# An attention and MLP kernel on one core: block 1's products during the first solve, merges interleaved on four row groups, values scaled on ScalarE, short solve steps fused

## Chip, core and metric

The kernel runs on one core of a Trainium2 chip. The metric is the device time of one execution in microseconds (us). TensorE (PE) multiplies, VectorE (DVE) and ScalarE (ACT) work on tiles elementwise, GpSimd (POOL) does the same on SBUF, and SyncE (SP) issues the DMAs.

## The reference, cut to what matters

Three layers one after the other: a delta-rule attention over 768 time steps for 4 batches of 8 heads of 48 numbers, a Fourier mixing with an MLP, and a gated MLP. The change touches the attention alone:

```python
k_n = k / (np.linalg.norm(k, axis=-1, keepdims=True) + 1e-06)
state = np.zeros((B, H, D, D))
for t in range(S):
    kt, vt, bt = k_n[:, :, t], v[:, :, t], beta[:, :, t, None]
    y[:, :, t] = np.einsum('bhd,bhde->bhe', q[:, :, t], state)
    v_old = np.einsum('bhde,bhd->bhe', state, kt)
    state = state + bt[:, :, :, None] * np.einsum('bhd,bhe->bhde', kt, vt - v_old)
```

## The kernel before

**Tiling.** Time is cut into 12 chunks of 64 steps for each of 4 batches: 48 chunks `bc`, in an order (`SEQ`) that staggers the batches by four. Two heads share the 128 partitions, so a chunk has four head pairs. Eight chunks make a block; there are six blocks. Inside a chunk the recurrence becomes a unit triangular system. Its inverse is made of two 32x32 triangles, inverted on DVE for a whole block at once (`solve`), and an off-diagonal 32x32 part made from two products on PE (`merge`).

**Stages of a chunk.** `stage_a` loads `kq` (448 KB), takes `k k^T` and `k q^T` on PE into PSUM (line 201), and moves them to the tile `gak`: ACT copies the `k k^T` half in two parts (`copy_g`, lines 191 and 192), DVE masks the `q` half (line 205). `stage_b` loads values `kv` and `qt`, scales the values by the norms of `k` on POOL (line 313), multiplies by the inverse `TT` (line 316) and copies the result to `WU` on ACT (line 321). `stage_c` forms `cw` (lines 332 and 333). `stage_d` takes the output and the new state (lines 345 and 347) and copies them on ACT (lines 358 and 362); it is the recurrence itself.

**Solve.** Line 219 forms `Cc` from the products, lines 226 and 232 scale it by mask and `d` (for blocks 1 to 5 line 226, the tile `dm`, runs on POOL), line 236 transposes it into `T`. Then 30 elimination steps follow, each of two products (line 252) and two additions (line 255) on halves of the rows. Line 271 scales, lines 275 to 277 transpose the result into `T1` and `Tc`. `norms` makes the inverse norms: for block 0 from squares summed on PE, for blocks 1 to 5 from a load `kn`, squared on ACT (line 142) and summed on DVE (line 144), then a root and eight small DVE operations (lines 146 to 153).

**Merge.** For eight head pairs a merge takes 16 products of 32x32 (line 291) into PSUM, ACT negates them into `zs` in two halves (line 296) and copies the diagonal blocks of `Tc` to `TT` (line 298); 16 more products (line 301) and two copies (line 303) complete `TT`. One merge serves two chunks; four merges make a block.

**Order.** The first solve is written out ahead of everything. While it runs, PE does 26 products of 128x512 that nothing reads (`busy(CF["keep"], 512)`, line 407). All later calls are events with a key in units of a chunk: they are emitted in that order with a priority, and a scheduler in the compiler, which simulates the program, sets the final order on each engine. `CF["pin"]` names operations that keep their place in program order. Block 1's `stage_a` may come no earlier than key -4, behind the first solve. The queue of SP is in order, and `kq` has five buffers. When the last solve is done, buffers of the attention are given up and the first weights of the MLP are loaded; the MLP stages follow.

```python
for j in range(1, NB):
    a0 = 8 * j - LM - NS - (8 + NA - 1) // NA
    at(max(a0 - CF["nl"], -LM), "N", norms, j)
```

Of the kernel before, what the change touches and what calls it, by code (L numbers as in the profile page):

```python
# [7 lines left out]
F32 = mybir.dt.float32  # L8
# [12 lines left out]
C = 64  # L21
# [23 lines left out]
    kq=5, kv=2, mb=2, cvd=3, cve=2, kn=4, sv="hhhhhd", pin=574,  # L45
    warm=10, keep=26, dfs=2, tn=2, early=4, ahead=1,
# [14 lines left out]
class Kernel:  # L61
    def __init__(self, tc, a):
        self.tc, self.nc, self.a, self.first = tc, tc.nc, a, None
# [10 lines left out]

    def load(self, out, in_):

        ins = self.nc.sync.dma_start(out=out, in_=in_)
        if self.first is not None:
            dep = mybir.DependencyInfo(mybir.DependencyClass.NoSync, mybir.DependencyReason.DATA)
            self.tc.add_manual_dep(ins.ins, self.first.ins.name, dep, reason="issue order")  # L80
        return ins
# [13 lines left out]
    def attention(self, cp, pg, pe, p, x, filler, after_solves):  # L95
# [17 lines left out]

        def norms(blk):
            if blk in normed:
                return
            normed.add(blk)
            s = slice(blk * 32, blk * 32 + 32)
            n0 = pe.tile([128, 32], F32, name="n0")
            n1 = pe.tile([128, 32], F32, name="n1")  # L120
            if blk == 0:
                ss = self.bank("pc", [128, 32])
                for i in range(2):
                    k2 = pe.tile([128, 1056], F32, name="Ts", bufs=CF["mb"])[:112, :1024]
                    nc.scalar.activation(k2, gas["k"][i].rearrange("p a b c -> p (a b c)"), AF.Square)
                    for g in range(16):
                        for r, q in ROWS:
                            nc.tensor.matmul(
                                ss[q, i * 16 + g : i * 16 + g + 1], lhsT=k2[r, g * C : g * C + C], rhs=one[r], start=True, stop=True
                            )  # L130
            else:
                ss = pe.tile([128, 32], F32, name="ss")
                w = 32 // CF["kn"]
                if blk == 1:
                    kn1 = p.tile([128, 4, HP, GA], F32, name="gak", bufs=3).rearrange("p a b c -> p (a b c)")
                for i in range(0, 32, w):
                    if blk == 1:
                        kn = kn1[:, i * D : (i + w) * D]
                    else:
                        kn = pe.tile([128, w * D], F32, name="kn", bufs=2)  # L140
                    self.load(out=kn, in_=a["kn"][blk, :, i : i + w].rearrange("p w d -> p (w d)"))
                    self.pin(nc.scalar.activation(kn, kn, AF.Square), blk)
                    kn = kn.rearrange("p (w d) -> p w d", d=D)
                    self.pin(nc.vector.tensor_reduce(out=ss[:, i : i + w], in_=kn, axis=AX.X, op=ADD), blk)
            nc.scalar.sqrt(n0, ss)
            nc.vector.tensor_scalar_max(n0, n0, 1e-30)
            nc.vector.reciprocal(n1, n0)
            nc.vector.tensor_mul(n1, n1, ss)
            nc.vector.tensor_add(n1, n1, n0)
            nc.vector.tensor_scalar(out=n_all[:, s], in0=n1, scalar1=0.5, scalar2=1e-6, op0=MUL, op1=ADD)  # L150
            nc.vector.reciprocal(n1, n_all[:, s])
            nc.vector.tensor_mul(n0, n1, bt[:, s])
            nc.vector.tensor_mul(d_all[:, s], n0, n1)
# [39 lines left out]

        def stage_a(bc):
# [12 lines left out]
        def solve(blk, nsl):  # L207

            Cc = pe.tile([128, 32, 32], F32, name="Cc")
            dm = pe.tile([128, 32, 32], F32, name="dm")  # L210
            d = d_all[:, blk * 32 : blk * 32 + 32]
            dT = pe.tile([128, 32], F32, name="dT", bufs=2)
            if blk == 0:
                for i in range(4):
                    copy_g(both0(i, C), pairs0("k", i))
            gs = [gas[blk * 8 + h4 * 4, 4][:, :, :, C : 2 * C].rearrange("p a b c -> p (a b) c") for h4 in range(2)]
            n = 32 // len(gs)
            for i, g in enumerate(gs):
                nc.vector.scalar_tensor_tensor(
                    out=Cc[:, :, n * i : n * i + n].rearrange("p c g -> p g c"),  # L220
                    in0=g[:, :, 32:], scalar=mk[:, 3 * C : 3 * C + 1], in1=g[:, :, :32], op0=MUL, op1=ADD,
                )
            if blk == 0:
                norms(0)
            nc.vector.transpose(out=dT, in_=d)
            (nc.gpsimd if blk else nc.vector).tensor_tensor(
                out=dm,
                in0=mk[:, 3 * C + 2 :].unsqueeze(2).to_broadcast([128, 32, 32]),
                in1=d.unsqueeze(1).to_broadcast([128, 32, 32]),
                op=MUL,  # L230
            )
            nc.vector.tensor_mul(Cc, Cc, dm)
# [3 lines left out]
            self.pin(nc.vector.transpose(out=T, in_=Cc), 16 + blk)  # L236
# [19 lines left out]

            for k in range(1, 31):
# [9 lines left out]
            for i, op in enumerate(steps):  # L267
                if i and i * nsl // len(steps) != (i - 1) * nsl // len(steps):
                    yield
                outer(*op)  # L270
# [6 lines left out]
            nc.vector.transpose(out=T1[:, 16:], in_=Tr[:, 16:])  # L277
            Tts[blk] = (Tc, T1)

        def merge(g8):  # L280

            blk, o = g8 // 4, (g8 % 4) * 8
            Tc, T1 = Tts[blk]
            tt = TT[g8 % NTT]
            z = self.bank("pz", [128, 2, 8, 32])
            qs = [slice(32 * u, 32 * u + 32) for u in range(4)]
            lo, up = qs[::2], qs[1::2]
            ga = [gas[g8 * 2 + g // 4][:, g % 4] for g in range(8)]
            for g in range(8):
                for h in range(2):  # L290
                    nc.tensor.matmul(  # L291
                        z[up[h], 0, g], lhsT=ga[g][lo[h], C + 32 : 2 * C], rhs=T1[lo[h], :, o + g], start=True, stop=True
                    )
            zs = p.tile([128, 8, 32], F32, name="zs", bufs=2)
            for h in range(2):
                nc.scalar.mul(zs[up[h]], z[up[h], 0], -1.0)
            for us in up + lo:
                nc.scalar.copy(out=tt[us, :, us], in_=Tc[us, o : o + 8])
            for g in range(8):
                for h in range(2):  # L300
                    nc.tensor.matmul(z[lo[h], 1, g], lhsT=zs[up[h], g], rhs=tt[up[h], g, up[h]], start=True, stop=True)
            for h in range(2):
# [698 lines left out]
```

## Time and profile before

| | us |
|---|---|
| median of three runs | 953.75 |
| lowest and highest | 952.13, 956.86 |
| the profiled execution | 958.1 |
| its span, first to last instruction | 956.3 |
| PE busy | 915.2 (96%) |
| DVE busy | 562.6 (59%) |
| ACT busy | 405.6 (42%) |
| POOL busy | 204.5 (21%) |

The attention fills the span to about 348 us, the MLP layers the rest. Busy shares are means over stages with different limits. A busy PE is not a PE at its peak: the records of a product run until its modelled end. A product of 32-bit numbers shows as two records.

### The profile page before, as it was taken

The numbers are of one execution on the slowest core, as the hardware profiler recorded it, in microseconds if no ns is written. First come the engines' busy times: TensorE is split into PE (matmuls) and PEld (weight loads), VectorE is DVE, ScalarE is ACT, GpSimd is POOL, SyncE is SP. The second block draws the span as 40 slices with busy tenths as digits, with TensorE's granted clock in tenths as the row PEclk, the third lists the DMA queues.
The fourth block names the chain that finished last, engine by engine and source line by source line (L and its number), as shares of the span: only waits on it lengthen the run. The fifth ranks groups of instructions, "written<-read, shape, count | busy, mean of one in ns | idle before, by whom it ended". The sixth has DMA issues, their size and how long they took to land.

```text
span 956.3 us, 18756 instructions
## 1 busy us (share of the span) xinstructions
PE 915.2 (96%) x7360; PEld 865.5 (91%) x7360; DVE 562.6 (59%) x1675; ACT 405.6 (42%) x1002; POOL 204.5 (21%) x198
## 2 busy tenths in 40 slices
PE   7989879999998998999999999999999999999998
PEld 7468769989998987899999999999989999899898
DVE  3967999988887489774559522322273352443521
ACT  3156566868887655422225221111252342332421
POOL 2011022122115215422124100000072132132221
PEclk7878969979997999999999999999999999999999
DMA  9069935723353254000130000000020100000001
GB/s 251 11 168 237 241 102 150 205 80 85 94 164 89 56 175 168 1 1 1 40 128 32 1 1 1 1 1 17 25 75 8 43 1 25 25 1 25 25 1 50
DMA packets 51593, 67.11 MB, mean 70 GB/s; under 512 B 28945, under 2 KB 41970, under 8 KB 51506
## 3 DMA queue, kind: packets, MB, share of 16 engines
q1 hardware_dynamic: 51506, 65.92, 24.3%
q8 instruction: 58, 0.95, 0.4%
q14 instruction: 29, 0.24, 0.1%
HBM read 61.19 MB, written 4.72 MB: 69 GB/s over the span
## 4 chain that ended last, share of the span: by engine, by line
PE 73%; DVE 11%; ACT 5%; DMA 4%; issue 4%; POOL 2%; SPq 0%; ACTq 0%; POOLq 0%; DVEq 0%
PE bankY L665 13%; PE bankX L650 12%; PE bankX L758 10%; PE bankY L778 5%; PE bankX L744 5%; PE bankX L719 4%; PE bankY L345 3%; PE bankY L316 3%; PE bankY L332 3%; PE bankY L347 3%; PE bankX L201 2%; DMA w<-in_w_dram 2%; PE bankZ L291 2%; POOL w L583 2%; DVE Ts L255 2%
## 5 line engine op out<-in xcount | busy, mean ns | idle before, releaser
L650 PE MATMUL bankX<-uh,w 128*128 128x384 f32 x576 | 162.1, 343 | 2.5 <-ACT w L582 1.4
L665 PE MATMUL bankY<-w,hh 128*128 128x384 f32 x576 | 137.6, 340 | 2.1 <-POOL w L583 1.3
L656 DVE SCALAR_TENSOR_TENSOR hl<-bankX,hh 128x384 fp32r<-128x384 f32 x96 | 53.2, 554 | 139.7 <-ACT hh L655 139.6
L655 ACT ACTIVATE hh<-bankX 128x384 fp32r<-128x384 f32 x96 | 47.0, 489 | 173.5 <-PE bankX L650 173.4
L650 PEld LDWEIGHTS bankX<-uh,w 128*128 128x128 f32 x576 | 104.8, 188 | 5.8 <-ACT w L582 3.2
L665 PEld LDWEIGHTS bankY<-w,hh 128*128 128x128 f32 x576 | 102.8, 188 | 5.3 <-POOL w L583 3.0
L758 PE MATMUL bankX<-ws,vh 128*128 128x384 f32 x384 | 98.6, 337 | 0.0
L650 PE MATMUL bankX<-ul,w 128*128 128x384 f32 x288 | 97.1, 337 | 0.0
L665 PE MATMUL bankY<-w,hl 128*128 128x384 f32 x288 | 84.1, 339 | 1.8 <-DVE hl L656 1.8
L766 DVE TENSOR_TENSOR g<-bankX,bsb 128x384 f32<-128x384 f32 x32 | 17.8, 558 | 101.7 <-PE bankX L758 101.7
L313 POOL TENSOR_TENSOR gak<-gak,n_all 128x192 f32<-128x192 f32 x48 | 38.4, 805 | 181.5 <-DMA gak<-in_kv_dram 128.2
L255 DVE TENSOR_TENSOR Ts<-Ts,tm 128x110 f32<-128x110 f32 (+31 forms) x325 | 76.0, 270 | 0.9
L345 PE MATMUL bankY<-WU,gak 128*112 128x96 f32 (+1 forms) x384 | 72.8, 278 | 1.1 <-ACT x L362 1.0
L252 DVE TENSOR_TENSOR tm<-Ts 128x110 f32<-128x110 f32 (+31 forms) x325 | 70.3, 254 | 0.8
L758 PEld LDWEIGHTS bankX<-ws,vh 128*128 128x128 f32 x384 | 69.1, 188 | 0.0
L347 PE MATMUL bankY<-Sb,cw 112*112 112x96 f32 (+1 forms) x352 | 66.2, 271 | 2.1 <-DVE cw L333 2.1
L758 PE MATMUL bankX<-ws,vl 128*128 128x384 f32 x192 | 64.3, 337 | 0.0
L345 PEld LDWEIGHTS bankY<-WU,gak 128*112 128x112 f32 (+1 forms) x384 | 54.8, 185 | 3.5 <-ACT x L362 1.4
L665 PEld LDWEIGHTS bankY<-w,hl 128*128 128x128 f32 x288 | 52.8, 188 | 2.8 <-DVE hl L656 2.7
L769 POOL TENSOR_TENSOR gl<-g,gh 128x384 fp32r<-128x384 f32 x32 | 32.4, 1013 | 105.3 <-ACT gh L768 88.1
L650 PEld LDWEIGHTS bankX<-ul,w 128*128 128x128 f32 x288 | 54.2, 188 | 0.1
L321 ACT COPY WU<-bankY 64x384 f32<-64x384 f32 x96 | 45.3, 472 | 20.3 <-PE bankY L316 19.0
(164 smaller groups left out, 1917.1 us busy)
## 6 DMA issues: line engine op xcount, KB each, us to landing
kq<-in_kq_dram SPq DMA_DIRECT2D x40, 448.0 KB, 6.6
qt<-in_qt_dram SPq DMA_DIRECT2D x48, 196.0 KB, 2.7
gak<-in_kv_dram SPq DMA_DIRECT2D x48, 192.0 KB, 3.6
w<-in_w_dram SPq DMA_DIRECT2D x24, 384.0 KB, 8.4
out_dram<-ot SPq DMA_DIRECT2D x24, 192.0 KB, 2.0
kn<-in_kn_dram SPq DMA_DIRECT2D x16, 192.0 KB, 3.5
s<-in_wi_dram SPq DMA_DIRECT2D x6, 512.0 KB, 4.0
cvd<-in_ws_dram SPq DMA_DIRECT2D x12, 192.0 KB, 2.4
```

What stands on the lines that cost most here:

```text
L252: nc.vector.tensor_tensor(out=tm, in0=x.to_broadcast(sh), in1=y.to_broadcast(sh), op=MUL)
L255: nc.vector.tensor_add(o, o, tm)
L321: nc.scalar.copy(out=o_, in_=pb[hs])
L345: nc.tensor.matmul(pd[:m, hp], lhsT=ak[:, hp, :m], rhs=u[:, hp], start=True, stop=(c == 0))
L347: nc.tensor.matmul(pd[:m, hp], lhsT=cw[:, hp, :m], rhs=sb[:, hp], start=False, stop=True)
L650: nc.tensor.matmul(ph, lhsT=w1[f][i][:, c * 128 : c * 128 + 128], rhs=cur[k][:, c], start=(c + j == 0), stop=(c == 2 and j == 2))
L655: nc.scalar.activation(hh, ph, AF.Relu)
L656: nc.vector.scalar_tensor_tensor(out=hl, in0=ph, scalar=0.0, in1=hh.bitcast(F32), op0=MAX, op1=SUB)
L665: nc.tensor.matmul(acc[t], lhsT=hx[i][:, t * 128 : t * 128 + 128], rhs=w2[e][k], start=(e == 0 and j == 0), stop=(e == 11 and j == 2),)
L744: nc.tensor.matmul(pu, lhsT=wi[2 * c][i][:, f * 128 : f * 128 + 128], rhs=xT[hf][k][:, c], start=(c + j == 0), stop=(c == 2 and j == 2),)
L758: nc.tensor.matmul(pv, lhsT=vn[i][:, s, f * 128 : f * 128 + 128], rhs=ws[2 * s + hf][k], start=(s + j == 0), stop=(s == 5 and j == 2),)
L778: nc.tensor.matmul(po, lhsT=gt[i][:, f, t * 128 : t * 128 + 128], rhs=wo[f][k], start=(f + j == 0), stop=(f == 3 and j == 2),)
```

## The change

- `stage_a` of block 1 (chunks 8 to 15) and its sums of squares are emitted before the first solve's steps are finished; the sums come from PE as for block 0, with the squares taken on ACT from `kq`. Block 1's `q` half is copied unmasked by ACT; `mask_q` masks blocks 0 and 1 later on DVE, ordered behind the first solve's last transpose (`behind`), as are block 1's norm operations.
- The dummy products are 12 instead of 26 and stand behind block 1's products and sums.
- For blocks 2 to 5 one DVE operation masks and moves both halves (128x512) out of PSUM; `copy_g` is gone there. Norms of blocks 2 and 3, and of 4 and 5, are made together.
- The preparation of a solve forms `Cc` contiguously and scales it by `d` in one DVE operation; the strided access moves to the transpose. `dm` on POOL is gone.
- Solve steps 1 to 3 and 28 to 30 become one to three fused operations (`few`).
- `merge(g + 1, first, second)` issues the first product of merge `g + 1` and the second of merge `g` alternately; all merges share one PSUM bank, and `zs` is made by one ACT operation instead of two. The diagonal copies are a call of their own (`diag`).
- Values are scaled on ACT, one operation for each head pair, instead of one on POOL.

```diff
@@ CF
-    kq=5, kv=2, mb=2, cvd=3, cve=2, kn=4, sv="hhhhhd", pin=574,
-    warm=10, keep=26, dfs=2, tn=2, early=4, ahead=1,
+    kq=5, kv=2, mb=2, cvd=3, cve=2, kn=4, sv="hhhhhd", pin=60,
+    warm=10, keep=12, few=3, dfs=2, tn=2, early=4, ahead=1,
@@ stage_a
-            o = C if SEQ[bc][1] < HALF else 0
-            m = mk[:, o : o + C].unsqueeze(1).to_broadcast([128, HP, C])
-            copy_g(gas[bc][:, :, C : 2 * C], pa[:, :, C:])
-            self.pin(nc.vector.tensor_tensor(out=gas[bc][:, :, :C], in0=pa[:, :, :C], in1=m, op=MUL), 8 + bc // 8)
+            if bc < 16:
+
+                copy_g(gas[bc][:, :, C : 2 * C], pa[:, :, C:])
+                nc.scalar.copy(out=gas[bc][:, :, :C], in_=pa[:, :, :C])
+                if bc == 8:
+                    gas["ss", 1] = self.bank("pc", [128, 32])
+                k2 = pe.tile([112, HP, C], F32, name="sq", bufs=2)
+                nc.scalar.activation(k2, kq[:, :, C : 2 * C], AF.Square)
+                sums(gas["ss", 1], k2.rearrange("p a b -> p (a b)"), (bc - 8) * HP, HP)
+            else:
+                self.pin(nc.vector.tensor_tensor(out=gas[bc][:, :, : 2 * C], in0=pa, in1=mask_a(bc), op=MUL), 8 + bc // 8)
+
+        def mask_q(bc):
+            out = gas[bc][:, :, :C]
+            self.behind(nc.vector.tensor_tensor(out=out, in0=out, in1=mask_a(bc)[:, :, :C], op=MUL))
@@ solve
-            (nc.gpsimd if blk else nc.vector).tensor_tensor(
-                out=dm,
-                in0=mk[:, 3 * C + 2 :].unsqueeze(2).to_broadcast([128, 32, 32]),
-                in1=d.unsqueeze(1).to_broadcast([128, 32, 32]),
-                op=MUL,
-            )
-            nc.vector.tensor_mul(Cc, Cc, dm)
+            if blk < 2:
+                nc.vector.tensor_mul(Cc, Cc, mk[:, 3 * C + 2 :].unsqueeze(1).to_broadcast([128, 32, 32]))
+            nc.vector.scalar_tensor_tensor(
+                out=Cc, in0=Cc, scalar=-1.0, in1=d.unsqueeze(2).to_broadcast([128, 32, 32]), op0=MUL, op1=MUL
+            )
+            def few(k):
+
+                if k < 16:
+                    for c in range(k):
+                        nc.vector.scalar_tensor_tensor(
+                            out=T[:, k + 1 :, c], in0=T[:, k + 1 :, k], scalar=T[:, k, c : c + 1], in1=T[:, k + 1 :, c], op0=MUL, op1=ADD
+                        )
+                else:
+                    for r in range(k + 1, 32):
+                        nc.vector.scalar_tensor_tensor(
+                            out=T[:, r, :k], in0=T[:, k, :k], scalar=T[:, r, k : k + 1], in1=T[:, r, :k], op0=MUL, op1=ADD
+                        )
@@ merge
+        def merge(g8, first, second):
+
+            z0, z1 = zz[:, g8 % 2], zz[:, (g8 - 1) % 2]
+            T1, o = (Tts[g8 // 4][1] if first else None), (g8 % 4) * 8
+            tt = TT[(g8 - 1) % NTT]
             for g in range(8):
                 for h in range(2):
+                    if first:
+                        ga = gas[g8 * 2 + g // 4][:, g % 4]
+                        nc.tensor.matmul(z0[up[h], g], lhsT=ga[lo[h], C + 32 : 2 * C], rhs=T1[lo[h], :, o + g], start=True, stop=True)
+                    if second:
+                        zs = zss[g8 - 1]
+                        nc.tensor.matmul(z1[lo[h], g], lhsT=zs[up[h], g], rhs=tt[up[h], g, up[h]], start=True, stop=True)
+            if first:
+                zss[g8] = p.tile([128, 8, 32], F32, name="zs", bufs=2)
+                nc.scalar.mul(zss[g8], z0, -1.0)
@@ stage_b
-            n = n_all[:, bc * 4 : bc * 4 + 4].unsqueeze(2).to_broadcast([128, HP, D])
-            nc.gpsimd.tensor_tensor(out=kv[:, :, D:], in0=kv[:, :, D:], in1=n, op=MUL)
+            for hp in range(HP):
+                nc.scalar.activation(kv[:, hp, D:], kv[:, hp, D:], AF.Copy, scale=n_all[:, bc * 4 + hp : bc * 4 + hp + 1])
@@ attention, behind the first yield of the first solve
+        for i in range(4):
+            nc.scalar.copy(out=both0(i, 0), in_=pairs0("q", i))
+        upto(16)
+        busy(CF["keep"], 512)
         for _ in first:
             pass
```

On PE around the first solve's end, the kernel before has its dummy products (L388), then block 1's (L201), then the merges (L291, L301):

```order
L388 MATMUL bankY<-TT_84 128x512 x26
L201 MATMUL bankX<-kq 128x128 x16
L291 MATMUL bankZ<-T_470,gak 32x32 x16
L301 MATMUL bankZ<-TT_84,zs 32x32 x16
L291 MATMUL bankZ<-T_470,gak 32x32 x16
L301 MATMUL bankZ<-TT_85,zs 32x32 x16
L201 MATMUL bankX<-kq 128x128 x20
```

The kernel after, at the same place; `sq` are the squares of a block 1 chunk, L208 is its `stage_a` product and that of block 2:

```order
L208 MATMUL bankX<-kq 128x128 x4
L125 MATMUL bankY<-one,sq 64x1 x8
L433 MATMUL bankY<-TT_84 128x512 x12
L337 MATMUL bankZ<-T_698,gak 32x32 x16
L208 MATMUL bankX<-kq 128x128 x16
L337 MATMUL bankZ<-T_698,gak 32x32
L340 MATMUL bankZ<-TT_84,zs 32x32
```

Block 1's products and sums moved ahead of the dummy products, block 2's first products stand where block 1's were, and the two kinds of merge products alternate.

On ACT, at the same place before (L298 are the diagonal copies, which need the solved `Tc`; L142 squares loads of `kn`):

```order
L142 ACTIVATE gak<-gak 128x384 x4
L298 COPY TT_85<-Tc 32x8x32 x4
L145 ACTIVATE n_577<-ss 128x32
L142 ACTIVATE kn<-kn 128x384 x2
L298 COPY TT_84<-Tc 32x8x32 x4
```

And after (L326 are the diagonal copies, L216 the squares for block 1's sums, L147 the root of its norms, L343 `zs`, L357 the value scaling):

```order
L212 COPY gak<-bankX 128x4x64
L326 COPY TT_85<-Tc 32x8x32 x4
L216 ACTIVATE sq<-kq 112x256
L194 ACTIVATE gak<-bankX,mk 128x4x32
...
L147 ACTIVATE n_702<-bankY 128x32
L326 COPY TT_84<-Tc 32x8x32 x4
L343 ACTIVATE zs<-bankZ 128x256
L357 ACTIVATE gak<-gak,n_all 128x48 x8
```

The first diagonal copies moved ahead of the last chunk's squares and copies.

On ACT in the later attention, where no `stage_a` is left, before (L296 `zs`, L303 the last copies to `TT`):

```order
L296 ACTIVATE zs<-bankZ 32x256 x2
L321 COPY WU_87<-bankY 64x4x2x48 x2
L298 COPY TT_84<-Tc 32x8x32 x4
L358 COPY Sb_90<-bankY 48x4x48 x2
L362 COPY x_63<-bankY 64x384
L303 COPY TT_84<-bankZ 32x8x32 x2
```

And after, at the merge that follows block 3's first:

```order
L343 ACTIVATE zs<-bankZ 128x256
L347 COPY TT_84<-bankZ 32x8x32 x2
L402 COPY Sb_90<-bankY 48x4x48 x2
L406 COPY x_63<-bankY 64x384
L357 ACTIVATE gak<-gak,n_all 128x48 x4
L365 COPY WU_86<-bankY 64x4x2x48 x2
```

The value scaling stands on ACT now, between the merge's copies and those of the chunks.

## Rows read from the trace of the kernel before

**Rows 1.** Busy time by stage: start and end, length, each engine, granted PE clock, DMA
```profile
47.80:120.40 72.60, 60.34 (x664) 56.42 (x662) 55.65 (x196) 40.60 (x119) 8.72 (x12) 0.83 0.87 213
120.40:160.80 40.40, 34.74 (x455) 32.17 (x456) 39.19 (x157) 25.55 (x68) 10.79 (x11) 0.75 0.45 123
160.80:202.30 41.50, 40.56 (x558) 38.83 (x558) 40.59 (x155) 34.66 (x96) 8.89 (x10) 0.93 0.63 174
202.30:244.20 41.90, 41.16 (x539) 38.54 (x538) 35.30 (x140) 31.50 (x86) 9.87 (x9) 0.86 0.29 78
244.20:279.30 35.10, 35.05 (x524) 33.29 (x523) 29.44 (x70) 29.24 (x74) 5.24 (x9) 0.95 0.38 102
279.30:347.80 68.50, 63.99 (x746) 60.44 (x744) 46.50 (x128) 46.03 (x124) 20.90 (x20) 0.88 0.32 89
347.80:956.30 608.50, 596.77 (x3439) 576.26 (x3437) 284.20 (x701) 186.58 (x416) 134.70 (x114) 0.95 0.10 33
```

**Rows 2.** The chain of waits, 0 to 130 us: start, length, what
```profile
41.39 0.23 DVE tm L252 x2
...
42.46 0.20 DVE Ts L255
...
47.77 2.38 DVE gak L405 x4
...
118.61 1.80 DVE Tc L276
```

**Rows 3.** The DMA queue's timeline: start, length of the issues, what is loaded
```profile
10.77 3.21 SPq L77 DMA_DIRECT2D kq<-in_kq_dram  x5
...
55.77 1.79 SPq L77 DMA_DIRECT2D kq<-in_kq_dram  x4
```

**Rows 4.** DVE instructions by line and shape: busy us, mean ns, idle before
```profile
L205 DVE TENSOR_TENSOR gak<-bankX,mk 128x256 f32<-128x256 f32 x40 | 16.3, 418 | 12.3 <-ACT gak L192 12.0
L219 DVE SCALAR_TENSOR_TENSOR Cc<-gak,mk 128x512 f32<-128x512 f32 x12 | 13.4, 1117 | 10.8 <-ACT gak L192 10.8
...
L144 DVE TENSOR_REDUCE ss<-kn 128x8 f32<-128x384 f32 x16 | 8.6, 548 | 2.4 <-ACT kn L142 2.4
...
L236 DVE STREAM_TRANSPOSE Ts<-Cc 128x1024 f32<-128x1024 f32 x6 | 7.5, 1242 | 0.1
```

**Rows 5.** Timelines of DVE (first two) and POOL around 148 us
```profile
148.31 0.43 DVE L252 TENSOR_TENSOR tm<-Ts 128x88 f32<-128x88 f32 x2
148.66 2.15 DVE L255 TENSOR_TENSOR Ts<-Ts,tm 128x88 f32<-128x88 f32 x2
...
148.19 2.49 POOL L226 TENSOR_TENSOR dm<-mk,d_all 128x1024 f32<-128x1024 f32 x1 [3.38 <-DVE d_all L153]
```

**Rows 6.** PE's timeline at four places; in brackets idle time and its releaser
```profile
25.78 25.38 PE L388 MATMUL bankY<-TT 128*128 128x512 f32 x52
...
54.69 1.07 PE L291 MATMUL bankZ<-T,gak 32*32 32x32 f32 x32
...
121.28 1.10 PE L291 MATMUL bankZ<-T,gak 32*32 32x32 f32 x32 [6.06 <-DVE T L277]
...
234.04 0.69 PE L301 MATMUL bankZ<-TT,zs 32*32 32x32 f32 x32 [0.21 <-ACT zs L296]
```

**Rows 7.** ACT instructions by line: busy us, mean ns, idle before
```profile
L296 ACT ACTIVATE zs<-bankZ 32x256 f32<-32x256 f32 x48 | 18.0, 375 | 6.9 <-PE bankZ L291 6.3
L191 ACT ACTIVATE gak<-bankX,mk 128x128 f32<-128x128 f32 (+1 forms) x44 | 17.0, 386 | 15.1 <-PE bankX L201 9.8 <-issue 4.4 <-PE bankX L183 0.4
...
L192 ACT COPY gak<-bankX 128x128 f32<-128x128 f32 (+1 forms) x44 | 12.2, 278 | 0.0
...
L145 ACT ACTIVATE n<-ss 128x32 f32<-128x32 f32 x5 | 1.1, 229 | 3.5 <-DVE ss L144 3.4
```

**Rows 8.** Timelines of the DMA queue and of POOL: a value load and its first use
```profile
246.64 1.22 SPq L77 DMA_DIRECT2D gak<-in_kv_dram  x2
...
250.73 1.20 POOL L313 TENSOR_TENSOR gak<-gak,n_all 128x192 f32<-128x192 f32 x2 [6.25 <-DMA gak<-in_kv_dram]
```

More of the change, by code (lines that the diff above doesn't have):

```diff
@@ L73, in pin, with order, behind @@
         return ins
-    def load(self, out, in_):
[L77 to L81, printed above, removed]
+    def order(self, ins, first):
+        if first is not None:
+            dep = mybir.DependencyInfo(mybir.DependencyClass.NoSync, mybir.DependencyReason.DATA)
+            self.tc.add_manual_dep(ins.ins, first.ins.name, dep, reason="issue order")
+        return ins
+    def load(self, out, in_):
+        return self.order(self.nc.sync.dma_start(out=out, in_=in_), self.first)
+    def behind(self, ins):
+        return self.order(ins, self.solved)
     def bank(self, what, shape):
@@ L112, in attention, with sums @@
         normed = set()
+        def sums(ss, k2, g0, n):
+            for g in range(n):
+                for r, q in ROWS:
+                    nc.tensor.matmul(ss[q, g0 + g : g0 + g + 1], lhsT=k2[r, g * C : g * C + C], rhs=one[r], start=True, stop=True)
         def norms(blk):
@@ L116, in norms @@
                 return
[L117 to L129, printed above, removed]
-                            )
-            else:
[L132 to L141, printed above, removed]
+            if blk < 2:
+                nb, ss = 1, gas["ss", blk]
+            else:
+                blk -= blk % 2
+                nb, w = 2, 32 // CF["kn"]
+                ss = pe.tile([128, 64], F32, name="ss")
+                for i in range(0, 64, w):
+                    kn = pe.tile([128, w * D], F32, name="kn", bufs=2)
+                    self.load(out=kn, in_=a["kn"][blk + i // 32, :, i % 32 : i % 32 + w].rearrange("p w d -> p (w d)"))
                     self.pin(nc.scalar.activation(kn, kn, AF.Square), blk)
@@ L276, in solve @@
             nc.vector.transpose(out=Tc.rearrange("p g i -> p i g"), in_=T)
-            nc.vector.transpose(out=T1[:, 16:], in_=Tr[:, 16:])
+            last = nc.vector.transpose(out=T1[:, 16:], in_=Tr[:, 16:])
+            self.solved = self.solved or last
             Tts[blk] = (Tc, T1)
[L280 to L288, printed above, removed]
+        qs = [slice(32 * u, 32 * u + 32) for u in range(4)]
@@ L289, in merge @@
             for g in range(8):
                 for h in range(2):
[L291 to L298, printed above, removed]
@@ L300, in merge @@
+            if second:
+                zss.pop(g8 - 1)
                 for h in range(2):
-                    nc.tensor.matmul(z[lo[h], 1, g], lhsT=zs[up[h], g], rhs=tt[up[h], g, up[h]], start=True, stop=True)
-            for h in range(2):
-                nc.scalar.copy(out=tt[lo[h], :, up[h]], in_=z[lo[h], 1])
+                    nc.scalar.copy(out=tt[lo[h], :, up[h]], in_=z1[lo[h]])
         def stage_b(bc):
@@ L371, in upto @@
             while nxt[0] < min(n, NBC):
-                norms(nxt[0] // 8)
+                if nxt[0] >= 16:
+                    norms(nxt[0] // 8)
                 stage_a(nxt[0])
@@ L451, in attention @@
         for g in range(NBC // 2):
-            at(lead(2 * g, LM, 0.4), "M", merge, g)
+            key = lead(2 * g, LM, 0.4)
+            if g % 4 == 0:
+                at(key - 0.5, "M", merge, g, True, False)
+            at(key - 0.3, "M", diag, g)
+            at(key, "M", merge, g + 1, g % 4 < 3, True)
+        for t in range(16):
+            at(lead(t, LC + 1, 0.5), "S", mask_q, t)
+        at(-LM, "N", norms, 1)
         for t in range(NBC):
```

79 lines of the change are left out of this document (46 added, 33 removed).

## The prediction

> **What bounds the kernel now.** I read the busy time by stage first, with stages cut where VectorE (DVE) ends a solve [rows 1]. From 347.8 us on, TensorE (PE) is busy 596.77 of 608.5 us at a granted clock of 0.95 of full speed; the change does not touch that code, so it can only bring it forward. In the attention before it, DVE is busy 39.19 of 40.4 us and 40.59 of 41.5 us in the stages of solves 3 and 4: there DVE sets the pace, though PE is busy too. After solve 4 (202.3 us) DVE has room and PE has none (41.16 of 41.9, then 35.05 of 35.1). The weak stretch is 47.8 to 120.4: DVE is busy 55.65 of 72.6 us, so it idles 17 us although everything later hangs on its solves.
>
> The chain of waits says why [rows 2]: the first solve is done at 47.77, the transpose that ends the second only at 118.61 + 1.80 = 120.4. The DMA queue's timeline shows the reason [rows 3]: five loads of `kq` for block 1 are issued from 10.77, the next only from 55.77, because the products that free these buffers stand on PE behind the 26 dummy products that run beside the first solve [rows 6].
>
> **The change, part by part.** All sums go against the profiled execution (958.1 us, span 956.3). Its ratio to the median of the runs, 953.75, is 0.9955, and I scale by that at the end.
>
> *The first solve's end.* In the new order ScalarE (ACT) squares two `kq` chunks of block 1 ahead of the root that starts the norms, so that root waits for loads. In exchange PE takes the sums of squares first. I count the two as equal and take only the shorter steps off: a step of two products and two additions costs 0.23 + 0.25 us and becomes one to three independent fused operations at about 0.20 for the first [rows 2]. Six steps save 0 to 1.5 us, I take 1.2, and the masked halves that DVE takes in between cost 0.8. End near 47.4 instead of 47.8.
>
> *A new wait behind it.* The ACT order puts the diagonal copies, which wait for the solve, ahead of the square of the last block 1 chunk. PE needs that square for the last sums, and its 12 dummies come behind them. So the dummies do not run beside the solve but after it: 24 records at 25.38/52 = 0.49 us are 11.7 us [rows 6], twice that at half clock. The first merge product starts at about 47.4 + 1.5 (four copies at 0.375 [rows 7]) + 0.4 + 11.7 = 61, or up to 73, where it started at 54.69 before. DVE does not wait for it: it has 16 masks and the second solve's preparation to do, and the first new product it wants (block 2's) stands some twelve steps into the second solve. Hence I count it at nothing on the path, 0 to 12 for the range.
>
> *The second solve's end.* What DVE did in 55.65 us between the two ends [rows 1] shrinks or moves. Eight of 12 square reductions go at 0.548 (4.4). Five operations at 1.117 that form `Cc` with a strided output become three with a plain one: half of that to all of it, I take 0.75 (3.3 less). Block 2's eight norm operations move behind, at 0.2 (1.6), and so do about six steps of solve 3 at 0.48 (2.9). Masks: 20 at 0.418 and 2.38 for block 0 become 16 at about 0.30 from SBUF and eight over twice the columns at 0.65, between 0.42 and 0.84 (0.5 less) [rows 2, 4]. The strided read makes one transpose 0.65 dearer (1.24 to about 1.9, the 1.80 of the other strided transpose). The short steps give 1.2. That leaves 42.4 us. Waits for PE and DMA inside it: 0 to 17 (the idle time of before), I take 4. The second solve ends at 47.4 + 46.4 = 93.8, 26.6 us earlier. But part is only postponed: four reductions (2.2), four masks (2.6), two `Cc` (1.5), the norms (1.6), one scaling and transpose (3.1) and six steps (2.9), together 13.9. **Net lead: 13 us.**
>
> *Solves 3 and 4* run on a full DVE, so the lead is carried. Per block the wider masks cost 8 x 0.23 = 1.9 and the transpose 0.65; shorter steps, plain `Cc` and paired norms give back 1.2 + 0.7 + 0.8. Even. One thing leaves DVE for good: while GpSimd (POOL) forms `dm` from 148.19 for 2.49 us, a pair of DVE additions takes 2.15 us where the pair before it took 0.43 [rows 5]. The change has no `dm` on POOL and no value scaling. Four such blocks at 1.7 are 6.8 us over solves 3 to 6; later ones fall where PE limits, so I take 4, bounds 0 and 20. The Trainium skill (SBUF — State Buffer, Who interferes with whom) says that a DVE instruction with two SBUF inputs and a GpSimd instruction that reads SBUF exclude each other for the whole instruction. Its result is a rival below.
>
> *Merges.* A merge's products take 1.07 and 0.69 us for 32 records each [rows 6]. In 18 merges they are now interleaved: 64 records at the faster rate of 21.6 ns are 1.38 instead of 1.76, with 1.07 (full overlap) and 1.76 as ends. Before solve 4 this lies under DVE; behind it some 10 merges count, 0 to 7 us, and I take 10 x 0.38 less what ACT takes back, 2 us. The Trainium skill (TensorEngine Tiling (Array Packing), Instruction Overhead) speaks against it: about 60 cycles for each matmul whatever its width. An estimate by that page at the full clock is 64 x 25 ns = 1.6 us, a gain of 1.6 us over ten merges in place of 3.8.
>
> *ACT.* Value scaling comes to ACT as four operations on 128x48 for each chunk. No such row exists: 0.229 (128x32) to 0.386 (128x128 with a scale from memory), I take 0.23 as nearest in size [rows 7], 0.92 a chunk. Blocks 2 to 5 lose copies of 0.386 + 0.278, and one of two scalings of `zs` goes (0.375 a merge). Where no copies were left (from about 220) ACT gains 8 x 0.23 - 0.375 = 1.5 us for two chunks. It had 35.1 - 29.24 = 5.9 us idle for the four pairs of a block [rows 1]: used up. And ACT, unlike POOL, is what every PSUM tile waits for. If it reaches a scaling before the load has landed, it stands: the load is issued at 246.64, POOL starts on it at 250.73 [rows 8], 4.1 us. In the new order only some six ACT operations (2.25 at 0.375) lie between. So 0 to 1.85 us for each of 14 pairs behind solve 4; I take 0.57, **8 us lost**.
>
> Sum: 958.1 - 13 - 4 - 2 + 8 = 947.1; times 0.9955: **943**.
>
> **The rivals.**
>
> *ACT stands at each pair (slower).* Those 1.85 us at 14 pairs are 26 us against 13 + 4 + 2 = 19 gained: 958.1 + 7 = 965, scaled 961. It decides from 19/14 = 1.4 us a pair. For it: the gap above, and an ACT 83% busy in 244.2 to 279.3. Against: where ACT is late, the load has landed and the wait shrinks. Chance 0.17.
>
> *The lead is lost on PE.* The dummies behind the solve run at half clock, the value products start no earlier than before, and only PE's wait of 6.06 us for the second solve [rows 6] and little else is saved, with the ACT loss taking some of it: 957, scaled 952. In other words, early products without an earlier start. For it: the order. Against: DVE paces solves 3 and 4. Chance 0.22.
>
> *More than the lead.* By the mechanism of [rows 5], POOL's 43.5 us of busy time between 47.8 and 279.3 [rows 1] each time stop a DVE addition for their own length, and half of that falls where DVE paces. Then some 15 us come on top of the forecast: 932, scaled 928. That is the skill's exclusion at its full worth. Against: most POOL work is 0.5 us long, and PE takes over as the bound. Chance 0.18.
>
> **How the numbers follow.** Forecast 943 with chance 0.43, own range 934 to 951. Half a percent, about what a measurement of this kernel can tell from no change, is 4.8 us: under 949 is faster, over 958.5 slower. Faster: 0.18 + 0.43 less its upper edge (0.05) + a fifth of the PE rival = 0.60. Slower: the ACT rival, 0.17, and a little of the PE rival: 0.20. Same: 0.20. The range runs from between the first and the last rival, 927, to the ACT rival's 961; about one in ten lies beyond each end.
>
> **What would show it.** DVE busy nearly throughout from 47 to 94, the second `Tc` near 94 and the fourth near 185 instead of 202; the dummies behind the first solve; no DVE pair of 2 us; merges of 64 records in 1.4 us. If ACT idles on the value loads by more than 1.4 us a pair, I am wrong in sign; if the second `Tc` is later than 105, the sum fails at DVE's waits.

## The result, and the profile after

The changed kernel takes 965.5 us (961.8 to 967.8 in seven runs) where the kernel before takes 953.75. The ratio is 1.0119, 95% interval 1.009 to 1.0149: slower. The forecast was 943 and faster, and 965.5 lies above the range that ended at 961. The rival that ends nearest, 961 with ACT standing at the value loads, had the chance 0.17, and the runs below show that it holds only a part of the loss.

Its profiled execution took 961.84 us (span 960.0), the shortest of the seven, while the one before (958.1) lies above its median. So the two profiles differ by only 3.7 of the 11.8 us: they tell in which stage time goes, and what a part of the change costs is taken from the medians of the runs. Busy time by stage, cut again where a solve ends on DVE; columns as in [rows 1]:

```profile
48.80:98.50 49.70, 45.36 (x505) 35.60 (x503) 45.80 (x159) 26.47 (x80) 0.15 (x1) 0.88 0.74 177
98.50:169.90 71.40, 56.84 (x702) 53.55 (x702) 56.76 (x191) 50.73 (x145) 0.31 (x2) 0.93 0.65 171
169.90:202.50 32.60, 26.07 (x426) 24.88 (x426) 31.78 (x126) 26.04 (x80) 0.15 (x1) 0.79 0.42 111
202.50:245.10 42.60, 38.63 (x545) 36.25 (x544) 38.56 (x130) 33.60 (x99) 0.15 (x1) 0.96 0.31 81
245.10:282.20 37.10, 34.24 (x523) 31.84 (x522) 25.20 (x58) 34.86 (x102) 0.00 (x0) 1.00 0.34 88
282.20:351.00 68.80, 61.55 (x749) 58.27 (x748) 45.04 (x128) 52.57 (x156) 14.48 (x12) 0.95 0.34 95
```

The second solve ends at 98.7 instead of 120.4, near what was forecast (93.8). The stage of the third lasts 71.4 us where it lasted 40.4, and the lead of 22 us is a delay of 9 when it ends (170.8 against 161.6); the fourth ends at 202.7, where 185 was forecast and 202.3 was before. In the stage of the third solve DVE is busy 56.76 of 71.4. Between the first and the fourth solve's end DVE idles 49.7 - 45.80 + 71.4 - 56.76 + 32.6 - 31.78 = 19.4 us; by [rows 1] it was 72.6 - 55.65 + 40.4 - 39.19 + 41.5 - 40.59 = 19.1. The idle time did not go away; it moved behind the second solve. In the stage of the sixth solve ACT is busy 34.86 of 37.1, where it was 29.24 of 35.1, and PE is no longer full (34.24).

What DVE waits for behind the second solve, in its timeline:

```profile
96.81 1.87 DVE L310 STREAM_TRANSPOSE Tc<-Ts 128x1024 f32<-128x1024 f32 x1
...
100.71 0.55 DVE L142 TENSOR_REDUCE ss<-kn 128x8 f32<-128x384 f32 x1 [1.58 <-ACT kn L140]
...
107.18 0.55 DVE L142 TENSOR_REDUCE ss<-kn 128x8 f32<-128x384 f32 x1 [2.54 <-ACT kn L140]
109.92 0.55 DVE L142 TENSOR_REDUCE ss<-kn 128x8 f32<-128x384 f32 x1 [2.19 <-ACT kn L140]
...
113.21 0.23 DVE L156 TENSOR_TENSOR d_all<-n,n 128x64 f32<-128x64 f32 x1
...
119.84 0.27 DVE L279 SCALAR_TENSOR_TENSOR Ts<-Ts 128x30 f32<-128x30 f32 x1
```

The bracket is idle time and what ended it. Over the whole stage of the third solve (98.5 to 169.9) the view of waits puts the larger part of DVE's 14.6 idle us down to the squares (us in total, times, longest):

```profile
DVE ss L142 <- ACT kn L140: 9.5, 7, 2.5
DVE cw L377 <- PE bankY L376: 4.0, 4, 1.7
```

`d_all` of block 2, without which its `Cc` can't be scaled (line 247), is there at 113.4 only, and the third solve's first step follows at 119.84. In the kernel before it was there at 62.5. It is a 64-column row: the norms of blocks 2 and 3 are one piece of work, and it needs all eight `kn` loads. The DMA queue issues them like this:

```profile
10.02 2.17 SPq L84 DMA_DIRECT2D kn<-in_kn_dram  x2
...
78.87 0.35 SPq L84 DMA_DIRECT2D kn<-in_kn_dram  x1
...
79.90 0.40 SPq L84 DMA_DIRECT2D kn<-in_kn_dram  x1
...
88.86 2.57 SPq L84 DMA_DIRECT2D kn<-in_kn_dram  x2
...
101.29 0.35 SPq L84 DMA_DIRECT2D kn<-in_kn_dram  x1
...
105.24 0.57 SPq L84 DMA_DIRECT2D kn<-in_kn_dram  x1
```

Two early ones, since `kn` has two buffers, and then each when a sum on DVE has given a buffer back and the queue has come to it: the sixth is issued before the second solve ends, the seventh and eighth behind it. The loads are not all that delays the sums. The squares stand in ACT's queue too:

```profile
98.27 0.79 ACT L357 ACTIVATE gak<-gak,n_all 128x48 f32<-128x48 f32 x3 [1.83 <-DMA gak<-in_kv_dram]
...
106.62 0.52 ACT L140 ACTIVATE kn<-kn 128x384 f32<-128x384 f32 x1
...
107.45 1.90 ACT L357 ACTIVATE gak<-gak,n_all 128x48 f32<-128x48 f32 x8
109.37 0.52 ACT L140 ACTIVATE kn<-kn 128x384 f32<-128x384 f32 x1
```

The eighth load lands 4.0 us after its issue, at 109.2, and its square starts at once. The seventh lands 2.7 us after its issue, at 104.0, and its square starts only at 106.62, behind other work of ACT. Before the fifth square (100.17) ACT stood 1.83 us at a value load.

The value scaling on ACT, in the view of instructions by line (busy us, mean ns, idle time before):

```profile
L357 ACT ACTIVATE gak<-gak,n_all 128x48 f32<-128x48 f32 x192 | 47.8, 323 | 13.4 <-DMA gak<-in_kv_dram 13.0
```

### The profile page after: what moved, and what is told of

It is laid out like the page before. It is cut to its first block, busy times and chain, and to the rows that moved or that the text cites. A ratio compares the mean times of both kernels' runs of the same rounds, so it can differ in the third digit from the quotient of the medians.

```text
span 960.0 us, 18869 instructions
## 1 busy us (share of the span) xinstructions
PE 903.7 (94%) x7460; PEld 860.1 (90%) x7460; DVE 560.0 (58%) x1611; ACT 427.4 (45%) x1116; POOL 156.6 (16%) x145
## 4 chain that ended last, share of the span: by engine, by line
PE 68%; DVE 14%; DMA 8%; ACT 7%; issue 2%; SPq 1%; POOL 0%; ACTq 0%; DVEq 0%
PE bankY L714 13%; PE bankX L699 13%; PE bankX L807 10%; PE bankY L827 5%; PE bankX L793 5%; PE bankX L768 4%; DMA gak<-in_kv_dram 4%; DVE cvd L623 2%; DVE cvd L626 2%; PE bankY L376 2%; PE bankY L360 2%; PE bankX L208 2%; PE bankY L391 2%; ACT gak L357 2%; PE bankY L389 2%
## 5 line engine op out<-in xcount | busy, mean ns | idle before, releaser
L389 PE MATMUL bankY<-WU,gak 128*112 128x96 f32 (+1 forms) x384 | 70.4, 271 | 3.6 <-ACT x L406 3.6
L273 DVE TENSOR_TENSOR Ts<-Ts,tm 128x110 f32<-128x110 f32 (+26 forms) x264 | 59.3, 261 | 0.7
L270 DVE TENSOR_TENSOR tm<-Ts 128x110 f32<-128x110 f32 (+26 forms) x264 | 58.9, 260 | 0.9
L391 PEld LDWEIGHTS bankY<-Sb,cw 112*112 112x112 f32 (+1 forms) x352 | 50.1, 182 | 10.3 <-DVE cw L377 9.8
L376 PE MATMUL bankY<-gak,WU 128*112 128x112 f32 x352 | 46.3, 277 | 9.1 <-ACT WU L365 9.0
L360 PE MATMUL bankY<-gak,TT 128*128 128x96 f32 x384 | 53.6, 284 | 0.8 <-ACT xr L397 0.7
```

What stands on the lines that cost most here:

```text
L270: nc.vector.tensor_tensor(out=tm, in0=x.to_broadcast(sh), in1=y.to_broadcast(sh), op=MUL)
L273: nc.vector.tensor_add(o, o, tm)
L360: nc.tensor.matmul(pb[:, hp].rearrange("p t d -> p (t d)"), lhsT=tt[:, o + hp], rhs=kv[:, hp], start=True, stop=True)
L376: nc.tensor.matmul(pc[:, hp], lhsT=w[:, hp], rhs=ak[:, hp], start=True, stop=True)
L389: nc.tensor.matmul(pd[:m, hp], lhsT=ak[:, hp, :m], rhs=u[:, hp], start=True, stop=(c == 0))
L391: nc.tensor.matmul(pd[:m, hp], lhsT=cw[:, hp, :m], rhs=sb[:, hp], start=False, stop=True)
```

## The experiments

Theory N: the pair of norms makes the third solve late. Theory V: the value scaling on ACT costs. Theory D: the dummies behind the first solve cost. Every edit makes the scheduler set a new order on all engines. Two controls on the kernel before, at the end, moved its time by 1 and by 4 us, so differences of that size between two kernels are weak evidence. Ratios are to the kernel before.

**Values on POOL again.**

```diff
-            for hp in range(HP):
-                nc.scalar.activation(kv[:, hp, D:], kv[:, hp, D:], AF.Copy, scale=n_all[:, bc * 4 + hp : bc * 4 + hp + 1])
+            n = n_all[:, bc * 4 : bc * 4 + 4].unsqueeze(2).to_broadcast([128, HP, D])
+            nc.gpsimd.tensor_tensor(out=kv[:, :, D:], in0=kv[:, :, D:], in1=n, op=MUL)
```

> The changed kernel with the values scaled on POOL again, one operation a chunk; all else as changed. Theory V (ACT stands on the value loads: 13.4 us of idle time in front of the scalings and 47.8 us busy in them): time falls from 965.5 to 945-957, the wait in front of ACT's scalings is gone, and the stages behind the fourth solve get shorter by 3 us or more. Theory N (the lead is lost because the norms of blocks 2 and 3 wait together for eight kn loads, so the third solve starts late): time stays within 962-967 and the third solve still ends at about 170 us. Theory D (the 12 dummy products behind the first solve): unchanged, 962-967.

957.9 us, ratio 1.0047 (1.0022 to 1.0072): 7.6 of the 11.8 us, just short of what V expected (945 to 957). From the fourth solve's end to the sixth's it takes 71.7 us instead of 79.7, as V expected. The third solve still ends at 170.1, and the pair's norms are ready at 116.7, no earlier than with values on ACT. So V has a part, and it isn't all.

**Norms one block at a time.**

```diff
-                blk -= blk % 2
-                nb, w = 2, 32 // CF["kn"]
-                ss = pe.tile([128, 64], F32, name="ss")
-                for i in range(0, 64, w):
+                nb, w = 1, 32 // CF["kn"]
+                ss = pe.tile([128, 32], F32, name="ss")
+                for i in range(0, 32, w):
```

> The changed kernel with the norms of blocks 2 to 5 made one block at a time again (32 columns, four kn loads each). Theory N: DVE's idle time between the second solve's end and the third's first step (98.5 to 119.8 in the changed kernel, 8.9 us idle) shrinks to under 4 us, the third solve ends at 155-162 instead of 170, and the time falls to 952-958. Theory V: the third solve may come earlier, but the time stays within 962-967, as ACT holds the later stages. Theory D: unchanged.

953.7 us, ratio 1.0011 (0.9993 to 1.0029): 11.9 us come back. DVE's timeline in that run:

```profile
97.51 0.16 DVE L155 TENSOR_TENSOR d_all<-n,n 128x32 f32<-128x32 f32 x1
...
106.16 0.27 DVE L278 SCALAR_TENSOR_TENSOR Ts<-Ts 128x30 f32<-128x30 f32 x1
...
114.69 0.19 DVE L155 TENSOR_TENSOR d_all<-n,n 128x32 f32<-128x32 f32 x1
```

Block 2's norms are ready at 97.7, block 3's at 114.9, about where the pair was ready. Between the second solve's end and the third's first step DVE idles 1.0 us where it idled 8.9. The third solve starts 13.7 us earlier and ends at 156.4 instead of 170.8. N's forecast holds in each of its numbers.

**Both.** The two edits together.

> The changed kernel with both undone: values scaled on POOL, norms one block at a time. Theory N alone: same as the run with single norms (952-958). Theory V alone: same as the run with values on POOL (945-957). If both hold and add: 940-950, faster than the kernel before.

948.6 us, ratio 0.9961 (0.9935 to 0.9988): 16.9 us from the changed kernel, where the two parts alone add up to 19.5. Nearly additive, and now faster than before, though by less than the forecast.

**No dummies.** `keep=0` in place of 12.

> The changed kernel without the 12 dummy products that run behind the first solve from 52.0 to 65.1 us (nothing reads them). Theory D (they delay the first merge and with it everything): first merge product at about 53 instead of 65, first chunk's output copied near 72 instead of 82.8, time 952-957. Theories N and V: PE comes earlier here, but the second solve (98.5) and the third (170) do not, and the time stays within 961-968; the granted clock may be lower between 52 and 80 us.

965.25 us: nothing. D, which forecast 952 to 957, falls. In the changed kernel the dummies do stand behind the first solve, as its PE timeline shows,

```profile
52.02 13.07 PE L433 MATMUL bankY<-TT 128*128 128x512 f32 x24
65.02 1.08 PE L337 MATMUL bankZ<-T,gak 32*32 32x32 f32 x32
```

and without them the first chunk's output is copied at 73.4 instead of 82.8. But it is a balance of several things: the granted clock from 48 to 120 us is 0.78 instead of 0.91, and the second solve ends at 106.9 instead of 98.7. The third solve ends at 160.8, 10 us earlier than in the changed kernel, against what N and V expected, and the total still doesn't move: the fourth solve ends 3.4 us earlier, the fifth 3.7 us later. So an early third solve alone does not settle the time, and N rests on the run before, not on this one.

**Values on ACT in the kernel before.** The first edit the other way round, in the old kernel alone.

> The kernel before with one part of the change alone: values scaled on ACT, four operations a chunk; all else as before. Undoing this part in the changed kernel gave back 7.6 us (965.5 to 957.9), and with single norms 5.1 us (953.7 to 948.6). Theory V (the scaling on ACT costs by itself, by standing on the value loads and by its own time): 5 to 10 us slower than before, 958-963, with idle time in front of ACT's scalings that ends with a load. Rival (it costs only together with the early second solve, or only through the order the scheduler happens to give): within 2 us of before, 951-955.

971.5 us, ratio 1.019 (1.0166 to 1.0214): 18.6 us slower, nearly twice the upper end of what V expected. Two rows of it, by stage behind the fourth solve, and the waits of its scaling line:

```profile
202.30:245.00 42.70, 39.18 (x547) 36.30 (x545) 38.24 (x146) 39.12 (x118) 0.16 (x1) 1.00 0.30 81
245.00:285.00 40.00, 35.66 (x510) 33.48 (x506) 27.51 (x66) 36.39 (x105) 0.00 (x0) 0.96 0.29 75
```

```profile
L313 ACT ACTIVATE gak<-gak,n_all x192: 319/323/367, 66.5 to 338.6; 128x48 f32<-128x48 f32 x192
...
  DMA gak<-in_kv_dram: 9.7, 7
```

ACT is busy 75.5 of 82.7 us there, PE 74.8; before, PE was busy 41.16 of 41.9 and 35.05 of 35.1 [rows 1]. So PE is no longer full and ACT is as busy as PE; that ACT now sets the pace is read from these shares and not shown further. Only 9.7 us in all are waits for the load.

**No scaling at all.** Single norms, the scaling left out.

> The changed kernel with single norms and no scaling of the values by the norms at all (this part of the computation is left out), which bounds what the scaling can cost on any engine. With the scaling on ACT it took 953.7, on POOL 948.6. Theory V (ACT's time and its standing on loads are the cost, POOL's scaling is free): within 2 us of the run with POOL, 946.5-950.5. Theory X (POOL's scaling stops DVE while both run, as in rows 5): 3 us or more below the run with POOL, under 945.5.

937.1 us, ratio 0.9833: 16.5 us under the same kernel with ACT and 11.5 under the one with POOL. POOL's scaling isn't free, against V. The time is on X's side, but its mechanism, POOL stopping DVE, doesn't show. In the run with both edits undone it looks like this: POOL's scaling line (ns, min/median/max), then PE, then the end of DVE's chain of solve steps:

```profile
L356 POOL TENSOR_TENSOR gak<-gak,n_all x48: 502/534/7507, 69.1 to 312.8; 128x192 f32<-128x192 f32 x48
```

```profile
173.98 2.03 PE L359 MATMUL bankY<-gak,TT 128*128 128x96 f32 x8 [4.92 <-POOL gak L356]
```

```profile
172.75 0.44 DVE L269 TENSOR_TENSOR tm<-Ts 128x100 f32<-128x100 f32 x2
173.11 0.44 DVE L272 TENSOR_TENSOR Ts<-Ts,tm 128x100 f32<-128x100 f32 x2
```

An operation of half a microsecond lasts up to 7.5 us, from 166.42 to 173.9. It ends 0.4 us after DVE's unbroken row of solve steps, and PE, which waits 4.92 us for it, starts at 173.98. (Spans on POOL are rough by themselves; PE's start bears this one out.) It looks like the exclusion of [rows 5] with the roles changed: there POOL held up a pair of DVE additions for 1.7 us, here DVE holds up POOL. It is not always the row's end that frees POOL: with values on POOL and paired norms one operation lasted 8.16 us and ended inside a row. DVE itself isn't seen to be slowed by the scaling: the products and additions of its solve steps take 119.0 us with it on POOL and 119.6 without. How the rest of the 11.5 us arises, beyond this one wait of PE, wasn't followed.

**A quarter of the scaling on ACT.** `range(1)` in place of `range(HP)`, single norms.

> The changed kernel with single norms and only the first of each chunk's four scalings on ACT (three quarters of the scaling are left out, so the values are wrong); its wait for the value load stays. With all four the time was 953.7, with none 937.1. Theory W (the cost is ACT standing on the load, some 13 us of idle time in front of the scalings): 949-954. Theory B (the cost is ACT's own time, 48 x 0.96 us, since ACT is full behind the fourth solve: 40.2 of 45.0 us between 200 and 245): three quarters of the 16.5 us come back, 939-943.

944.9 us, between the two: 8.8 of the 16.5 us come back with three quarters of ACT's work, while the waits in front grow:

```profile
  DMA gak<-in_kv_dram: 20.6, 24
```

So ACT's own time is about half of the price at least, and the rest is its standing, or its last quarter; the two aren't told apart further.

**Values on DVE.** `nc.vector` in place of `nc.gpsimd`, with single norms and the four buffers below.

> The changed kernel with single norms, four buffers for their loads, and values scaled on DVE, one operation a chunk (943.5 with POOL). Theory X (on POOL a scaling stands up to 7.5 us while DVE runs its solve steps, and PE behind it; leaving the scaling out saved 11.5 us): no such standing here, but 48 operations of some 0.35 us on DVE and DVE's own waits for the loads, of which about half count: 935-943. Rival (DVE has no room and stands on the loads as ACT did): 946-955.

958.4 us, 14.9 more than with POOL, beyond what the rival expected: DVE stands on the loads as ACT did, 13.9 us in front of 15 of the 48 scalings. A better place for the scaling wasn't found.

**Merges not alternated**, on top of both edits.

```diff
-            at(key, "M", merge, g + 1, g % 4 < 3, True)
+            at(key, "M", merge, g + 1, False, True)
+            if g % 4 < 3:
+                at(key, "M", merge, g + 1, True, False)
```

> The changed kernel with single norms and values on POOL (948.6 us), and besides the two kinds of merge products no longer alternated: the second product of a merge is issued whole, then the first of the next. In the trace of the changed kernel 64 alternated records take 1.09 us, against 1.07 + 0.69 apart, so PE should be busy 18 x 0.67 = 12 us more. Theory PE (behind the fourth solve PE sets the pace, so some ten merges count): 5-8 us slower, 953-957. Theory DVE or ACT (other engines set the pace there too): within 2 us, 946.5-950.5.

949.6 us, ratio 0.9959 (0.9942 to 0.9975), against 948.6: not told apart. The products do overlap fully, as the changed kernel's PE timeline shows at its second merge (first and last of the 64 records, 69.80 to 70.89):

```profile
69.80 0.22 PE L337 MATMUL bankZ<-T,gak 32*32 32x32 f32 x1
...
70.59 0.30 PE L337 MATMUL bankZ<-T,gak 32*32 32x32 f32 x4
```

But the some 12 us that this takes off PE can't be seen in the time.

**Four buffers for the norms' loads**: `bufs=4` for `kn`, in four kernels. On both edits undone:

> The changed kernel with single norms and values on POOL (948.6 us), and four buffers for the loads that the norms are made from instead of two. In the single-norms runs block 2's norms are ready at 97.5 and 103.2 us, where in the kernel before they were ready before 100 and the third solve had done six steps when the second ended. Theory N carried on (the third solve still waits for these loads): block 2's norms ready by 90, third solve ended at 150-156 instead of 162.7, time 940-946. Rival (DVE has no room left, the loads no longer matter): third solve at 158-164, time 946.5-950.5.

943.5 us, ratio 0.9897 (0.9873 to 0.9921): the best complete kernel, faster than both. Norms of block 2 at 87, third solve at 156.6. On the changed kernel whole:

> The changed kernel whole (norms of two blocks together, values on ACT), with four buffers in place of two for the loads that the norms are made from. Theory N1 (the pair is dear because its eight loads pass through two buffers, each given back only when DVE has summed it): block 2's norms ready at 95-105 instead of 113.2 us, third solve ended by 162 instead of 170.9, time 953-960. Theory N2 (the pairing itself, eight sums on a full DVE, is dear whatever the buffers): 962-967.

959.0 us, ratio 1.0061 (1.0027 to 1.0095): 6.5 us back with the pair kept, though the runs spread from 952.9 to 969.6. Its norms are ready at 107.1 instead of 113.4, and the third solve ends at 165.3, both later than N1 expected. So the loads in front of the pair are a part of its price. They may not be all of it: the next run differs from this one by single norms alone, and takes 954.1, though 5 us is hardly more than an order can make. With single norms and values on ACT:

> The changed kernel with single norms and four buffers for their loads, values on ACT as changed. With values on POOL the same kernel took 943.5. Theory V (ACT's scaling costs more than POOL's also here): 947-953. Rival (once the loads come in time the place of the scaling no longer matters): 941.5-945.5.

954.1 us, 10.6 more than with POOL: V again. Against the same kernel with two buffers (953.7) the four buffers bring nothing here. In the kernel before, as a control:

> The kernel before with four buffers in place of two for the loads that the norms are made from; nothing else. A control for the runs with four buffers. Theory: in the kernel before the third solve has its norms long before it starts, so the loads cost nothing there: 951-955. Rival (more buffers help any of these kernels): 943-949.

957.2 us, ratio 1.0041 (1.0015 to 1.0067): 4 us slower, which neither side expected.

**A new order alone.** The kernel before with 25 dummies.

> The kernel before with 25 dummy products in place of 26; nothing reads them, but the scheduler makes its order anew. A control for how far a new order alone moves the time: four buffers for the norms' loads, which should have been free there, cost 4 us. Theory S (a new order alone moves this kernel by 3 us or more, so differences of that size between any two of these kernels say nothing): 956 or above, or 950 or below. Rival (orders are worth under 2 us): 951-955, and the 4 us belong to the buffers.

954.8 us, ratio 1.0016 (0.9999 to 1.0033): Theory S is not borne out by this one order. Whether the 4 us above come from the norms, which were ready only 2 to 3 us earlier there, or from the order that run had, isn't shown.

**Norms still earlier**, in the best kernel: `max(a0 - CF["nl"], -LM)` as in the kernel before.

> The fastest complete kernel so far (single norms, values on POOL, four buffers for the norms' loads: 943.5), with the norms of block 2 allowed to come four chunks earlier, as in the kernel before. Theory N (the third solve still waits for its norms): norms ready by 75 instead of 86.8, third solve ended before 155, time 938-942. Rival (the norms are early enough by now): 941.5-947.

949.0 us, 5.5 slower than with the later start: the rival's side and beyond it. The norms are ready at 62.9, yet the third solve ends at 157.7, no earlier than with norms at 86.9, so theory N fails here. The fourth solve ends earlier than in the best kernel (193.6 against 198.2) and the sixth at nearly the same time (263.2 against 262.5); the loss comes behind that, and why isn't shown.

## Why the prediction was wrong

**The step that failed** is in "Solves 3 and 4": they "run on a full DVE, so the lead is carried", paired norms entered as 0.8 us of DVE instructions given back, and the balance was "Even". Waits of DVE were priced up to the second solve's end only: 4 us taken, 49.7 - 45.80 = 3.9 measured. Behind it they were put at nothing, and there DVE idles 14.6 us, 9.5 of them in front of sums for the paired norms. The postponed work was counted, 13.9 us of it, but as work that DVE does back to back. What the pair waits for was not priced: block 2's norms can't be made before block 3's loads have come, through two buffers that DVE itself frees, and have been squared on a busy ACT. Making the norms one block at a time brought back 11.9 us (965.5 to 953.7), nearly the whole net lead of 13. I named DVE's waits as the place where the sum could fail, but put the mark at the second solve's end (105), one stage too early. (In the sum for that end the masks come to 0.7 less, not 0.5; nothing hangs on it.)

One part of the change the prediction doesn't mention at all: block 2's norms may come no earlier than key 0, where they could come from key -4 before (`max(a0 - CF["nl"], 0)` for `max(a0 - CF["nl"], -LM)`). With single norms and four buffers the earlier key brought nothing; whether it would have made the pair cheap was not run.

**The ACT term** was 8 us lost and the POOL term 4 won, so a net 4 for moving the scaling. Moving it back gave 7.6, 5.1 and 10.6 us in three settings of the changed kernel, and moving it alone cost the kernel before 18.6. Against no scaling at all ACT's price is 16.5 us, twice the term. The mechanism was wrong as well. The term was ACT standing at loads behind the fourth solve, 0.57 us for each of 14 pairs. Of the 13.0 us of standing only this falls there (us, times; from 202.5 us on):

```profile
  DMA gak<-in_kv_dram: 2.8, 4
```

That is 0.2 us a pair; the other 10.2 us fall before. About half of the price or more is ACT's own time, where it is 34.86 of 37.1 us busy. By my own mark, 1.4 us of standing a pair, the sign should have been right: 13.4 us over all 24 pairs are 0.56. The mark looked at the standing alone. The 5.9 us "idle for the four pairs, used up" was read rightly and then not carried on to that end.

**The POOL term** was 4 us won by taking POOL's work away. Left out altogether, the scaling saves 11.5 us against POOL; so it was dear there too. One wait of 4.92 us of that is shown, POOL standing behind DVE; that POOL stopped DVE isn't seen in the run with both edits undone. The Trainium skill (SBUF — State Buffer, Who interferes with whom) says that of two such instructions the one that comes first holds the shared port and the other stops for all of it. The runs agree, and add that POOL's operation lasted 7.5 us, far beyond one DVE instruction of about 0.26.

**Right were** the new order behind the first solve (the dummies from 52.0, first merge at 65.0, forecast 61 or up to 73), that this costs nothing on balance (965.25 without them), the early second solve with its 4 us of waits, and the absence of DVE pairs of 2 us. The first solve ended at 49.7, not 47.4: `Cc` is now formed behind the norms (1.37 us for two operations), where before it was formed while they were awaited, its transpose reads with a stride (1.91 us for 1.25), and the fused steps save next to nothing. The first six operations take

```profile
25.22 1.32 DVE L279 SCALAR_TENSOR_TENSOR Ts<-Ts 128x30 f32<-128x30 f32 x6
```

and the three steps that they replace went from 23.73 to 25.09 before; the last six take 1.16 us where three steps took 1.34.

**Merges**: 1.09 us for 64 records, the end of the range called full overlap, not the 1.38 that I took. Their 2 us on the path could not be told from nothing. The estimate of 1.6 by the Trainium skill (TensorEngine Tiling (Array Packing), Instruction Overhead) counted each record as a matmul. The kernel issues 32 matmuls here, and by the same 60 cycles of the Trainium skill (25 ns at the full clock) the estimate would be 0.8 us. The measured 1.09 us lies above it, so these runs don't speak against the Trainium skill.

Without scaling and with single norms the kernel takes 937.1; the sum without its ACT term is (958.1 - 13 - 4 - 2) x 0.9955 = 934.9. That is near, but the terms were not checked apart, and errors in them may cancel: the POOL term holds only 4 of the 11.5 us that leaving POOL's scaling out is worth. Open remain how ACT's price divides between standing and work, how the pair's price divides between its loads, ACT's queue and the later key, and why two kernels with earlier norms were slower.

## What to carry to other kernels

A result that is made for two consumers at once is as late as the inputs of the later one: before joining small operations, look at the loads, buffers and queue behind each half, and price the first consumer's wait. Work moved to an engine is priced in the stage where that engine has the least room, and by what its in-order queue will stand on; an ACT 83% busy (29.24 of 35.1 us) was the fullest engine once 1.0 us a chunk (47.8 us for 48) came to it. An idle time that is closed in one stage can open in the next if the work behind it isn't ready: sum the idle time over both, here 19.1 us before and 19.4 after.

## What the runs showed of the hardware that was not expected

A POOL operation of 0.5 us on SBUF lasted 7.5 us beside an unbroken row of DVE operations with two inputs and ended 0.4 us after the row; another lasted 8.16 us and ended inside a row. 32 products of 32x32 (64 records) on alternating row groups took 1.09 us, about as long as 16 (32 records, 1.07 us) on one pair of groups. A DVE transpose of 128x1024 with a strided read takes 1.93 us against 1.24 plain [rows 4]; moving the stride from `Cc` to it made each of the two operations that form `Cc` 0.74 instead of 1.12 us.
